# One written order of 340 steps for attention and the first two experts

## The chip, the cores and the metric

The kernel runs on one core of a Trainium2 chip. A core has five engines, each with its own queue of instructions: TensorE (PE, matmuls; its weight loads are shown as PEld), VectorE (DVE), ScalarE (ACT), GpSimd (Pool) and SyncE (SP). Sixteen DMA engines move data between the chip's memory and the core; Pool and SP start the transfers here. The metric is device time in microseconds (us), from the first to the last instruction of the run, median of several runs.

## The reference

Two operators in a row. First an attention without a score matrix, for 8 batches, 8 heads, 576 tokens and 64 dimensions a head:

```python
q_s = softmax(q, axis=-1)            # over the 64 dimensions
k_s = softmax(k, axis=2)             # over the 576 tokens
kv  = einsum('bhsd,bhse->bhde', k_s, v)
x   = einsum('bhsd,bhde->bhse', q_s, kv)   # then laid out as 4608 tokens x 512
```

Then a mixture of 8 experts over the 4608 tokens. Each token has one expert, fixed by its id; an expert is two matrices, 512 x 1024 and 1024 x 512:

```python
expert_idx = token_ids * 2654435761 % 8
for e in range(8):
    xe = x[expert_idx == e]
    out[expert_idx == e] = maximum(xe @ w1[e], 0) @ w2[e]
```

## The kernel before

**Slots.** Each expert has 640 slots of tokens: 72 for each of the 8 batches (columns 0 to 575), and 64 more (columns 576 to 639) for overflow, tokens of any batch that did not fit. DVE, PE and Pool first work out which token stands in which slot. Then the query rows of an expert are fetched in slot order, so that attention is computed already sorted by expert: five gathers of 128 rows (`raw`, L357, indices `gidx`), an exponential on ACT for each (`expq`, L368, into `qs`), sums and scales on DVE (`sums`, L380 to L386), transposes on PE (`turned`, L396) with a copy out of PSUM (L401, into `qT`), and products with the batch's key-value matrix `kvr` (`product`, L410) with a copy into the expert's input `XTp` or `X` (L413 on DVE, L415 on ACT). The overflow rows take the same way by indices `oidx`, with `xov` (L426) and a spread over the experts (`shared`, L436 to L444, into `XTov`).

**Keys and values.** For each batch SP loads `kraw` (L673), Pool loads `v` (L677, converted to 16 bits on the way); ACT takes the exponential of k (`expk`, L320) and fills v's extra columns with ones (`mark`, L324); PE makes 72 small matmuls (`keys`, L334); DVE scales the result into `kvr` (`scaled`, L341 to L347).

**An expert.** Its weights come in two halves for each matrix (`fetch`, L456). `first` (L471) makes steps of two blocks of 128 hidden units on some range of token columns, each followed by a relu on ACT into `hT` (L474); `second` (L482) makes a block of 128 tokens, DVE copies it to `ob` (L485), and Pool scatters its rows to the output (L488).

**Buffers.** Three `kraw`, four `v`, two k exponentials, ten `raw`, two `qs` sets, two weight sets, four `ob`. PSUM is held in three pairs: T for `keys`, `second` and overflow; Q for transposes and products; S (two banks each) for `first` and the spread.

**Order.** The block runs under a manual schedule for Pool, PE, DVE and ACT: every engine executes its instructions in the order in which the program names them. Expert 0 stands among the attention steps, its first matmul in three column ranges (0 to 288, 288 to 432, 432 to 640) as batches come. Experts 1 to 7 run in a loop, where small pieces for later experts are put after numbered steps by `_Slots`: softening of expert e+2, products of the next pair, exponentials of expert e+3. The gather of expert 3's queries is named after expert 0's last scatter, and its exponentials right behind:

```python
            for blk in range(3, BPE):
                moe.second(0, wts, hT, blk, opool, sl.side)
            qs[3] = gather(3)
            at.expq(qs[3], 0, 5)
```

Of the kernel before, what the change touches and what calls it, by code (L numbers as in the profile page):

```python
# [43 lines left out]
class _Index:  # L44
# [30 lines left out]
    def core(self, cpool, wait):  # L75
# [46 lines left out]
        A = ipool.tile([128, NCH, CELL], F16)  # L122
# [54 lines left out]
    def counts(self, cpool, fpool):  # L177
# [20 lines left out]
        flag = fpool.tile([128, 1], I32)  # L198
# [12 lines left out]
        return flag  # L211
# [17 lines left out]
    def onehot(self):  # L229
        V, Z = self.nc.vector, self.Z  # L230
        AO = self.ipool.tile([128, NCH, OVF], F16)
        V.tensor_tensor(out=AO[:], in0=self.rowi[:, 1:1 + OVF].unsqueeze(1).to_broadcast([128, NCH, OVF]),
                        in1=Z[:, 2, :].unsqueeze(2).to_broadcast([128, NCH, OVF]), op=ALU.is_equal)
        self.AO = AO

# [34 lines left out]
    def rows(self, cpool):  # L270
        nc, V = self.nc, self.nc.vector
        p2 = self.ps.tile([128, 512], F32, tag="T")
        for e in range(E_MOE):
            for n in range(NBP):
                nc.tensor.matmul(p2[64:128, 2 * e:2 * e + 2], lhsT=self.Qs[n][:, OVF * e:OVF * e + OVF],
                                 rhs=self.part[:, n, :], start=(n == 0), stop=(n == NBP - 1))
        u = slice(64, 128)
# [11 lines left out]
class _Attention:  # L289

    def __init__(self, nc, tc, q, k, v, cpool, qpool, ps):
# [11 lines left out]
        self.turn = 0  # L303
# [3 lines left out]
    def clear(self, lo, hi):  # L307
        for b in range(lo, hi):
            self.nc.vector.memset(self.kvrs[b][:], 0.0)

    def fill(self, ix):
        V = self.nc.vector
        V.tensor_scalar(out=self.ident[:], in0=ix.rowi[:, 0:128], scalar1=ix.pidf[:, 0:1], scalar2=None,
                        op0=ALU.is_equal)
        for i in range(2):
            V.memset(self.q16s[i][64:128, BPE - 1], 1.0)
# [33 lines left out]
    def gather(self, idx, widths):  # L350
        nc = self.nc
        q16 = self.q16s[self.turn % 2]
        self.turn += 1
# [36 lines left out]
    def turned(self, rq16, i, dst, act=False):  # L390
        nc = self.nc
        q16, w = rq16[1], rq16[2][i]
        pq = self.ps.tile([128, 512], F32, tag="Q")
        pv = pq[:].bitcast(F16).rearrange("p (r t) -> p r t", r=8)[:, 0:NPAIR, :]
        for r in range(NPAIR):
            nc.tensor.transpose(pv[:, r, 0:w], q16[0:w, i, 2 * r:2 * r + 2, :].rearrange("p h d -> p (h d)"),  # L396
                                self.ident[0:w, 0:w])
        if act:
            nc.scalar.copy(dst, pv[:, :, 0:w])
        else:  # L400
            nc.vector.tensor_copy(dst, pv[:, :, 0:w])  # L401

    def product(self, qT, XTp, r, lo, hi, es, q0=0):
# [8 lines left out]
        if r % 2:  # L412
            nc.vector.tensor_copy(XTp[:, es, r, lo * CELL:hi * CELL], pv)  # L413
        else:
            nc.scalar.copy(XTp[:, es, r, lo * CELL:hi * CELL], pv)  # L415

    def overflow(self, n, qTo, tpool):
# [7 lines left out]
        xov = tpool.tile([128, D_MOE], F16, name=f"xov{n}")  # L425
        nc.vector.tensor_copy(xov[:], pt[:])  # L426
        return xov

    def shared(self, xovs, Qs):
        nc = self.nc  # L430
        for h in range(2):
            pr = self.ps.tile([128, 2, 512], F32, tag="S")
            for i in range(2):
                r = 2 * h + i
                for n in range(NBP):
                    nc.tensor.matmul(pr[:, i, :], lhsT=xovs[n][:, r * 128:(r + 1) * 128], rhs=Qs[n][:],  # L436
                                     start=(n == 0), stop=(n == NBP - 1))
            for i in range(2):
                dst = self.XTov[:, :, 2 * h + i, :]
                src = pr[:, i, :].rearrange("p (e i) -> p e i", e=E_MOE)  # L440
                if i:
                    nc.scalar.copy(dst, src)
                else:
                    nc.vector.tensor_copy(dst, src)  # L444


class _Moe:
# [15 lines left out]
    def first(self, e, w, XTp, hT, lo, hi, side):  # L463
        nc = self.nc
        w1r = w[0][:].rearrange("p (c f) -> p c f", c=DC)
        for f2 in range(FC // 2):
            ph = self.ps.tile([128, 2, 512], F32, tag="S")
            for i in range(2):
                fc = 2 * f2 + i
                for dc in range(DC):  # L470
                    nc.tensor.matmul(ph[:, i, :hi - lo], lhsT=w1r[:, dc, fc * 128:(fc + 1) * 128],  # L471
                                     rhs=XTp[:, e % 2, dc, lo:hi], start=(dc == 0), stop=(dc == DC - 1))
            hv = hT[:, 2 * f2:2 * f2 + 2, lo:hi]
            nc.scalar.activation(hv, ph[:, :, :hi - lo], ACT.Relu)  # L474
            side()

    def second(self, e, w, hT, blk, opool, side):
# [3 lines left out]
        for fc in range(FC):  # L481
            nc.tensor.matmul(po[:], lhsT=hT[:, fc, blk * 128:(blk + 1) * 128], rhs=w2r[:, fc, :],  # L482
                             start=(fc == 0), stop=(fc == FC - 1))
        ob = opool.tile([128, D_MOE], F32, tag="ob")
        nc.vector.tensor_scalar(out=ob[:], in0=po[:], scalar1=1.0 / SX, scalar2=None, op0=ALU.mult)  # L485

        def scatter():
            sc = nc.gpsimd.indirect_dma_start(  # L488
                out=self.out[:, :],
                out_offset=bass.IndirectOffsetOnAxis(ap=self.ix.sidx[:, e, blk:blk + 1], axis=0),  # L490
                in_=ob[:], in_offset=None, bounds_check=N_TOK - 1, oob_is_err=False)
            self.tc.declare_no_dep(sc.ins, group="scatter", reason="each row is in one slot")
            self.tc.add_to_no_dep_group("scatter", sc.ins)
        scatter()
        side()
# [121 lines left out]

class _Slots:
# [21 lines left out]
def kernel(  # L640
# [10 lines left out]
    nc = tc.nc  # L651
    fpool = ctx.enter_context(tc.tile_pool(name="flag", bufs=1))
    with ExitStack() as fctx:
# [3 lines left out]
        xpool = P("xt", 2)  # L657
        qpool = P("q")
        wa = P("w16a", reuse_waits="tile")
        hpool = P("h")  # L660
        opool = P("o", 4)
        actx = ExitStack()
        tpool = P("tab", c=actx, side="right")
# [4 lines left out]

        kraws, v16s = {}, {}

        def load_k(b):
            kraws[b] = apool.tile([128, NPAIR * C9 * DH_], F32, tag="kraw", name=f"kraw{b}", bufs=3)
            nc.sync.dma_start(kraws[b][:], k[b])  # L673

        def load_v(b):
            v16s[b] = apool.tile([128, NPAIR * C9, VW], F16, tag="v16", name=f"v16_{b}", bufs=4)
            nc.gpsimd.dma_start(v16s[b][:].rearrange("p c d -> p (c d)"), v[b])  # L677

        QW = [128] * (BPE - 1) + [MAINC - 128 * (BPE - 1)]
        eng = mybir.EngineType  # L680
        with tc.manual_schedule(engines={eng.Pool, eng.PE, eng.DVE, eng.Activation}):
            at = _Attention(nc, tc, q, k, v, cpool, qpool, ps)
            at.clear(0, 4)
# [7 lines left out]
            gather = lambda e: at.gather(ix.gidx[:, e, :], QW)  # L691
            k16s, pkvs = {}, {}
            qT = qpool.tile([128, NPAIR, 4, MAINC], F16)

# [5 lines left out]
            def mark(b):  # L700
                at.mark(v16s[b])

            def keys(b):
                pkvs[b] = at.keys(k16s[b], v16s[b])

            def scaled(b):
                at.scaled(b, pkvs[b], apool)

            def turned(rq, e, i):
                at.turned(rq, i, qT[:, :, e % 4, 128 * i:128 * i + QW[i]])  # L710

            def turned_o(n):
                at.turned(qo, n, qTo[:, :, n * 128:(n + 1) * 128])

            ix.core(cpool, lambda: at.clear(4, 6))
            q0 = gather(0)
            load_v(2)
            load_v(3)
            expk(0)
            mark(0)  # L720
            keys(0)
            expk(1)
            at.clear(6, 8)
            flag = ix.counts(cpool, fpool)
            ix.overflow()
            scaled(0)
            ix.onehot()
            mark(1)
            keys(1)
            expk(2)  # L730
            at.expq(q0, 0, 3)
            scaled(1)
            po = ix.find()
            at.expq(q0, 3, 5)
            mul = at.sums(q0, 0, 3)
            ix.found(po, oidx, tpool)
            qo = at.gather(oidx, [128] * NBP)
            wts = moe.new_weights(wa)
            moe.fetch(wts, 0, 1)
            load_v(4)  # L740
            at.fill(ix)
            mul()
            Qs = ix.onehots(tpool)
            for i in range(3):
                turned(q0, 0, i)
            mark(2)
            keys(2)
            expk(3)
            ix.rows(cpool)
            at.soften(q0, 3, 5)  # L750
            scaled(2)
            load_v(5)
            moe.fetch(wts, 0, 2)
            for i in range(3, 5):
                turned(q0, 0, i)
            mark(3)
            keys(3)
            expk(4)
            at.expq(qo, 0, 4)
            scaled(3)  # L760
# [175 lines left out]
```

## Time and profile before

| | |
|---|---|
| runs | 272.69, 273.97, 274.76 us; median 273.97 |
| span of the profiled run | 270.1 us |
| busy: PE, PEld, DVE, ACT, Pool | 201.0, 131.8, 151.2, 102.9, 115.5 us |
| bytes moved by DMA | 51.42 MB, mean 190 GB/s |
| last key product (`keys`) | starts at 81.6 us |
| first matmul of expert 2 | at 145.8 us |

Engines overlap, so the busy times don't add up to the span. In the page's slices a digit is the busy share of one fortieth of the span in tenths; PEclk is the clock that PE was granted, in tenths. An idle time "[9.47 <-DMA raw]" is the time that the engine stood idle before this instruction, with what released it.

### The profile page before, as it was taken

The page shows a single profiled execution, that of the slowest core. Times are in us where ns is not written, and L with a number is a line of the kernel's source. Part 1 is how long each engine was busy: PE and PEld are TensorE (multiplying, and loading weights), DVE is VectorE, ACT ScalarE, POOL GpSimd, SP SyncE. Part 2 cuts the span into 40 slices and gives each one's busy share as a digit, 9 for nine tenths or more (in the row PEclk, how much of TensorE's full clock was granted, in tenths as well). Part 3 has the DMA queues.
Part 4 walks back from the last instruction along what each step waited for, and adds up shares of the span by engine and source line. Part 5 has one row for each costly group of instructions (what it writes and reads, how often), then busy time and mean ns, then how long its engine had stood idle before and what let it go on. Part 6 is the DMA issues. An engine that isn't in the chain of part 4 may idle for free. (4 is left out here: it accounts for less than half of the span.)

```text
span 270.1 us, 4969 instructions
## 1 busy us (share of the span) xinstructions
PE 201.0 (74%) x1987; PEld 131.8 (49%) x1987; DVE 151.2 (56%) x303; ACT 102.9 (38%) x159; POOL 115.5 (43%) x140
## 2 busy tenths in 40 slices
PE   2436084497925677707989999959999989999990
PEld 2435073275605525404656746635755745746640
DVE  8994747766279439416357846645954855022031
ACT  2334264155540343034435526525625532622500
POOL 5170393232741000487135857743874333434051
PEclk9999999999997579975999999999999999999999
DMA  6999989999996000179922997993798892793032
GB/s 251 312 343 372 285 244 305 258 212 287 217 291 178 0 4 0 65 184 197 274 84 91 179 275 220 201 293 123 147 226 298 159 223 100 141 227 134 27 115 73
DMA packets 13548, 51.42 MB, mean 190 GB/s; under 512 B 2504, under 2 KB 2504, under 8 KB 12496
## 3 DMA queue, kind: packets, MB, share of 16 engines
q0 software_dynamic: 12224, 41.58, 61.7%
q1 hardware_dynamic: 1296, 9.47, 9.1%
q8 instruction: 17, 0.28, 0.4%
q14 instruction: 11, 0.09, 0.1%
HBM read 63.25 MB, written 10.49 MB: 273 GB/s over the span
## 5 line engine op out<-in xcount | busy, mean ns | idle before, releaser
L488 POOL DMA_INDIRECT out_dram<-ob,sidx x40 | 40.2, 1005 | 99.0 <-DVE ob L485 95.6
L482 PE MATMUL po<-w2r,hT 128*128 128x512 f16 x320 | 73.4, 379 | 0.4 <-DVE kvr L347 0.4
L471 PEld LDWEIGHTS <-w1r 128*128 128x128 f16 x544 | 52.9, 101 | 34.7 <-issue 11.6
L474 ACT ACTIVATE hT<-ph 128x640 f16<-128x640 f32 (+3 forms) x68 | 45.5, 671 | 49.7 <-PE ph L471 49.6
L485 DVE TENSOR_SCALAR ob<-po 128x512 f32<-128x512 f32 x40 | 27.7, 692 | 57.3 <-PE po L482 54.3
L357 POOL DMA_INDIRECT raw<-in_q_dram,gidx x40 | 45.0, 1124 | 29.2 <-DVE row L162 7.9
L471 PE MATMUL ph<-X,w1r 128*128 128x320 f16 x384 | 54.5, 299 | 0.0
L482 PEld LDWEIGHTS <-hT 128*128 128x128 f16 x320 | 30.2, 98 | 32.5 <-issue 0.4
L368 ACT ACTIVATE qs<-raw 128x512 f16<-128x512 f32 (+1 forms) x44 | 26.5, 627 | 37.7 <-DMA raw<-in_q_dram,gidx 35.2
L380 DVE TENSOR_REDUCE rq<-qs 128x16 f32<-128x1024 f16 (+1 forms) x18 | 26.1, 1449 | 17.6 <-ACT qs L368 17.6
L471 PE MATMUL ph<-XTp,w1r 128*128 128x320 f16 (+3 forms) x160 | 24.2, 311 | 13.6 <-ACT hT L474 9.7
L396 PE MATMUL pq<-ident,qs 128*128 128x128 f16 (+1 forms) x176 | 17.2, 234 | 17.2 <-DVE qs L386 15.8
L386 DVE TENSOR_TENSOR qs<-qs,rq 128x1024 f16<-128x1024 f16 (+1 forms) x18 | 26.2, 1458 | 0.4
L334 PE MATMUL pt<-v,k 64*64 64x65 f16 x576 | 15.0, 223 | 13.5 <-ACT v L324 7.3
L396 PEld LDWEIGHTS <-qs 128*128 128x128 f16 (+1 forms) x176 | 13.1, 107 | 22.2 <-ACT v L324 10.2
L410 PE MATMUL px<-qT,kvr 128*128 128x144 f16 (+1 forms) x160 | 15.0, 232 | 9.4 <-ACT X L415 3.1
L334 PEld LDWEIGHTS <-k 64*64 64x64 f16 x576 | 14.4, 137 | 14.6 <-issue 13.7
L401 DVE COPY qT<-pq 128x512 f16<-128x512 f16 (+1 forms) x40 | 14.7, 389 | 9.7 <-PE pq L396 9.4
L320 ACT ACTIVATE k<-kraw 128x2304 f16<-128x2304 f32 x8 | 17.0, 2122 | 6.4 <-DMA kraw<-in_k_dram 4.5
L410 PEld LDWEIGHTS <-kvr 128*128 128x128 f16 x160 | 11.5, 108 | 14.4 <-issue 9.4
L415 ACT CAST X<-px 128x432 f16<-128x432 f32 (+1 forms) x18 | 8.6, 477 | 21.7 <-PE px L410 21.7
L413 DVE CAST X<-px 128x432 f16<-128x432 f32 (+1 forms) x18 | 9.9, 551 | 4.4 <-PE px L410 4.4
(103 smaller groups left out, 120.6 us busy)
## 6 DMA issues: line engine op xcount, KB each, us to landing
kraw<-in_k_dram SPq DMA_DIRECT2D x8, 1152.0 KB, 10.8
w1r<-in_moe_w_dram POOLq DMA_DIRECT2D x16, 512.0 KB, 7.3
w2r<-in_moe_w_dram POOLq DMA_DIRECT2D x16, 512.0 KB, 10.8
v<-in_v_dram POOLq DMA_DIRECT2D x8, 594.0 KB, 16.9
raw<-in_q_dram,gidx POOLq DMA_INDIRECT x40, 10.1
out_dram<-ob,sidx POOLq DMA_INDIRECT x40, 2.8
raw<-in_q_dram,oidx POOLq DMA_INDIRECT x4, 7.4
ids<-in_moe_token_ids_dram SPq DMA_DIRECT2D x1, 36.0 KB, 1.7
```

The source lines that it names most:

```text
L334: nc.tensor.matmul(pkv[s, r, 0:DH_ + 1], lhsT=k16[s, r * C9 + c, :], rhs=v16[s, r * C9 + c, 0:DH_ + 1], start=(c == 0), stop=(c == C9 - 1))
L357: nc.gpsimd.indirect_dma_start(out=raw[0:w, :], out_offset=None, in_=self.q[:, :], in_offset=bass.IndirectOffsetOnAxis(ap=idx[0:w, i:i + 1 ...
L368: self.nc.scalar.activation(q16[0:w, i].rearrange("p h d -> p (h d)"), raws[i][0:w, :], ACT.Exp)
L380: nc.vector.reduce_sum(rv, qv, axis=AX.X)
L386: nc.vector.tensor_tensor(out=qf, in0=qf, in1=rv.rearrange("p i h -> p (i h)").unsqueeze(2) .to_broadcast([w, (hi - lo) * H_, DH_]), op=AL ...
L396: nc.tensor.transpose(pv[:, r, 0:w], q16[0:w, i, 2 * r:2 * r + 2, :].rearrange("p h d -> p (h d)"), self.ident[0:w, 0:w])
L410: nc.tensor.matmul(pv[:, :, i * CELL:(i + 1) * CELL], lhsT=self.kvrs[b][:, r, :], rhs=qT[:, r, q0 + es.start:q0 + es.stop, b * CELL:(b + 1 ...
L471: nc.tensor.matmul(ph[:, i, :hi - lo], lhsT=w1r[:, dc, fc * 128:(fc + 1) * 128], rhs=XTp[:, e % 2, dc, lo:hi], start=(dc == 0), stop=(dc = ...
L474: nc.scalar.activation(hv, ph[:, :, :hi - lo], ACT.Relu)
L482: nc.tensor.matmul(po[:], lhsT=hT[:, fc, blk * 128:(blk + 1) * 128], rhs=w2r[:, fc, :], start=(fc == 0), stop=(fc == FC - 1))
L485: nc.vector.tensor_scalar(out=ob[:], in0=po[:], scalar1=1.0 / SX, scalar2=None, op0=ALU.mult)
L488: sc = nc.gpsimd.indirect_dma_start(out=self.out[:, :], out_offset=bass.IndirectOffsetOnAxis(ap=self.ix.sidx[:, e, blk:blk + 1], axis=0), ...
```

## The change

All of attention and of experts 0 and 1 is cut into named steps, and one list gives their order; each engine executes its part of the list. A name tells the step: EK, MK, KV, SC are `expk`, `mark`, `keys` and `scaled` of a batch; V a load of v; G a gather (GO of the overflow rows); EQ an exponential of one query tile; SM and ML the sum and the scale; TP and TC a transposed tile and its copy; PP and PC a product and its copy; XP and XC the overflow product and its cast; SH and SD the spread; OV the overflow columns of a pair; W a weight matrix; A and R a step of `first` and its relu; B, C and S a block of `second`, its copy and its scatter. CNT, OVA, OHA, FND, FDD, QS, ROP and ROD make the index of the overflow.

What it is for: work of one expert can stand between pieces of another, so that an engine that waits for one has the other. Both experts now have their first matmul in two column ranges, 0 to 288 and 288 to 640. v's third load stands ahead of the first gather, the gathers of experts 2 and 3 follow each other, the overflow gather is named before the sums of expert 0, and DVE reaches its index without them. Copies of transposed tiles of experts 0, 1 and the overflow, the overflow casts, and the clearing of `kvr` and `qs` move from DVE to ACT. The second weight set and its pool are there from the start. Experts 2 to 7 keep their loop.

```diff
-    def clear(self, lo, hi):
-        for b in range(lo, hi):
-            self.nc.vector.memset(self.kvrs[b][:], 0.0)
+    def clear(self):
+        nc = self.nc
+        zero = self.cpool.tile([128, 1], F16, name="zero")
+        nc.vector.memset(zero[:], 0.0)
+        for b in range(B_):
+            nc.scalar.copy(self.kvrs[b][:].rearrange("p r d -> p (r d)"), zero[:].to_broadcast([128, NPAIR * 128]))
+        for i in range(2):
+            nc.scalar.copy(self.q16s[i][64:128, BPE - 1].rearrange("p h d -> p (h d)"),
+                           self.two[64:128, 0:1].to_broadcast([64, D_MOE]))
...
+ORDER = """
+EK0 MK0 V2 CNT KV0 G0 EK1 OVA SC0 MK1 KV1 OHA EK2 V3 V4 SC1 FND MK2 FDD KV2 EK3 QS GO EQ0_1 ROP SC2 EQ0_0 EQ0_2
+EQ0_3 SM0a EQ0_4 EK4 W01 ROD V5 ML0a G1 SM0b TP0_2 TP0_1 TC0_2 TC0_1 TP0_0 MK3 ML0b TC0_0 KV3 TP0_4 SC3 EK5 V6
+TP0_3 V7 W02 TC0_4 MK4 W11 PP0_00 TC0_3 KV4 PC0_00 EQO_0 W12 EQO_1 PP0_01 SC4 EK6 PP0_03 SMOa EQO_3 EQO_2 PC0_01
+MLOa PP0_02 G2 PC0_02 SMOb TPO_0 TCO_0 TPO_1 PC0_03 XP0 TCO_1 MLOb A0_0_1 XC0 A0_0_3 R0_0_1 TPO_3 R0_0_3 TPO_2
+A0_0_0 MK5 EQ1_0 KV5 EQ1_1 R0_0_0 EQ1_4 EQ1_3 A0_0_2 SC5 EK7 XP1 SM1b MK6 ML1b XC1 KV6 R0_0_2 EQ1_2 MK7 G3 SM1a
+TCO_3 KV7 TCO_2 ML1a TP1_3 TP1_4 TC1_3 TC1_4 SC6 TP1_2 TP1_1 TC1_2 SC7 TC1_1 XP2 TP1_0 XC2 PP0_40 XP3 TC1_0
+PC0_40 B0_0 XC3 PP1_01 C0_0 PP1_41 SH1 PC1_01 S0_0 PC1_41 PP0_42 SD1 PP1_42 SH0 PC1_42 PC0_42 PP0_43 SD0 PP0_41
+B0_1 EQ2_0 PC0_41 OV0 EQ2_1 PC0_43 EQ2_2 PP1_02 C0_1 PP1_00 EQ2_3 A0_288_0 SM2a S0_1 PC1_02 EQ3_1 A0_288_2 EQ3_2
+ML2a PC1_00 PP1_03 R0_288_2 PP1_43 R0_288_0 A0_288_1 PC1_43 EQ3_3 PC1_03 TP2_2 EQ3_0 OV1 TP2_0 R0_288_1 TC2_2
+A1_0_2 TC2_0 EQ3_4 SM3a A0_288_3 R1_0_2 EQ2_4 PP1_40 W21 A1_0_0 R0_288_3 ML3a TP2_1 PC1_40 G4 B0_2 R1_0_0 TC2_1
+SM2b A1_288_3 TP3_1 R1_288_3 C0_2 TP3_0 B0_3 ML2b TC3_1 A1_288_0 C0_3 S0_2 TC3_0 TP2_4 SM3b R1_288_0 S0_3 PP2_03
+B0_4 TC2_4 ML3b PP2_02 W22 A1_288_1 PC2_02 PC2_03 TP3_2 C0_4 R1_288_1 TP2_3 A1_0_1 TC3_2 EQ4_3 S0_4 TC2_3 EQ4_4
+PP2_01 TP3_3 EQ4_2 PC2_01 A1_0_3 TC3_3 R1_0_1 PP2_00 TP3_4 R1_0_3 A1_288_2 TC3_4 PC2_00 EQ4_0 PP2_61 PP2_60
+R1_288_2 PC2_61 B1_0 EQ4_1 PC2_60 PP2_62 C1_0 PP2_30 PC2_62 B1_2 PC2_30 S1_0 PP2_31 C1_2 PP2_32 B1_3 PC2_31
+PC2_32 S1_2 PP2_33 C1_3 PP2_63 B1_1 PC2_33 S1_3 PC2_63 B1_4 C1_1 S1_1 C1_4 S1_4
+""".split()
...
+                            A(qTo[:, :, i * 128:(i + 1) * 128], pq[e, i])
+                        else:
+                            (A if e < 2 else V)(qT[:, :, e % 4, 128 * i:128 * i + QW[i]], pq[e, i])
...
+                (V if r % 2 else A)(X[:, es, r, lo * CELL:hi * CELL], px[e, r, lo])
+
+            for e, es, parts in ((0, slice(0, 1), ((0, 4), (4, 8))), (1, slice(1, 2), ((0, 4), (4, 8))),
+                                 (2, slice(0, 2), ((0, 3), (3, 6), (6, 8)))):
...
+            for e in (0, 1):
+                for lo, hi in ((0, 288), (288, CAP)):
...
+            for name in ORDER:
+                st.run(name)
...
-            qs[3] = gather(3)
-            at.expq(qs[3], 0, 5)
...
-            for e in range(1, E_MOE):
-                wts = wn
...
+            for e in range(2, E_MOE):
+                h, w = hs[e % 2], wts[e]
```

Here A stands for ACT's copy and V for DVE's.

## The prediction

> **What bounds the kernel now.** I read the page's busy row and slices first, then the busy table by stages, then the waits of PE in the stage with the holes, and last the order of time on ACT and Pool around the largest hole. The chain of waits is no help: it holds only the last 0.7 us.
>
> ```profile
> PE 201.0 (74%) x1987; PEld 131.8 (49%) x1987; DVE 151.2 (56%) x303; ACT 102.9 (38%) x159; POOL 115.5 (43%) x140
> PEclk9999999999997579975999999999999999999999
> DMA  6999989999996000179922997993798892793032
> ```
>
> No engine is full over the span, and DMA has a hole of zeros where PE's clock is also down. So the stages differ. Cut at the points where the work changes:
>
> ```profile
> 0.00:57.00 57.00, 26.02 (x511) 22.32 (x512) 41.63 (x112) 19.51 (x22) 23.86 (x40) 1.00 0.97 292
> 57.00:69.00 12.00, 10.07 (x215) 7.18 (x214) 7.81 (x19) 6.83 (x9) 3.82 (x6) 1.00 1.05 256
> 69.00:84.00 15.00, 8.45 (x191) 6.60 (x190) 8.23 (x14) 6.54 (x12) 8.38 (x9) 0.90 1.04 255
> 84.00:146.00 62.00, 43.11 (x310) 26.54 (x308) 32.07 (x59) 21.08 (x40) 19.11 (x20) 0.83 0.37 99
> 146.00:270.00 124.00, 113.33 (x768) 69.19 (x766) 61.45 (x102) 48.97 (x77) 60.35 (x66) 1.00 0.70 175
> ```
>
> Columns: window, length, busy PE, PEld, DVE, ACT, Pool, granted clock, DMA share, GB/s. Until 84 us the 16 DMA engines are full (0.97 to 1.05): that stage is DMA-bound. From 84 to 146 DMA is at 0.37 and PE has 18.9 us of idle time, with a clock of 0.83: neither is full, so this is a stage of bad order. From 146 (experts 2 to 7) PE is 91% busy at full clock. Which waits make the 18.9 us:
>
> ```profile
> PE ph L471 <- ACT hT L474: 9.7, 1, 9.7
> PE pq L396 <- DVE qs L386: 1.8, 1, 1.8
> PE ph L471 <- DVE XTp L826: 1.7, 1, 1.7
> ```
>
> One wait is half of it. PE waits for a relu; the relu's own queue shows why it is late, and Pool shows why its blocker is late:
>
> ```profile
> 116.76 0.63 ACT L368 ACTIVATE qs<-raw 128x512 f16<-128x512 f32 x1 [9.47 <-DMA raw<-in_q_dram,gidx]
> 122.56 1.27 ACT L474 ACTIVATE hT<-ph 128x640 f16<-128x640 f32 x2
> ```
>
> ```profile
> 109.99 0.98 POOL L488 DMA_INDIRECT out_dram<-ob,sidx  x1 [26.63 <-DVE ob L485]
> 111.95 0.98 POOL L488 DMA_INDIRECT out_dram<-ob,sidx  x1 [0.98 <-DVE ob L485]
> 113.24 1.05 POOL L357 DMA_INDIRECT raw<-in_q_dram,gidx  x1 [0.30 <-issue]
> ```
>
> The five exponentials of expert 3's queries stand in ACT's order ahead of expert 1's relus; their gather stands in Pool's order behind the scatters of expert 0's last two blocks, which wait for their results. So Pool sat 26.6 us while DMA was idle, then ACT 9.5 us for the gather, then PE 9.7 us for ACT.
>
> [...] after the hole from 113.6 to 123.3 the clock is 0.50 until 128, and 32 matmuls of 320 columns take 7.21 us, against 48 in 6.68 us later. [...]
>
> **The change, part by part.**
>
> 1. *Loads reordered.* Bytes are the same; what counts is what stands ahead of the last attention batch. Cost per load, in time of all 16 engines: the SP queue has 9.1% of 270.1 us for eight k loads, 24.6 us. In the stretch from 50 to 58 us almost only weights move, at about 215 GB/s, so a half of 0.52 MB is 2.45 us and a matrix 4.9. The two late stages (0.37 x 62 = 22.9 us; 0.70 x 124 = 86.8 us) hold 4 and 20 halves, 2 and 3 gathers of five, about 1.4 and 6 sets of five scatters, and some 1.5 us of earlier work; solved, a gather set costs about 2 us and a scatter set about 5. The 82 us before 84 then leave 27 us for the eight v loads. The new Pool order puts ahead of v's last load: v 27, k 24.6, gathers of expert 0, overflow and expert 1 6, w1 of expert 0 4.9: 62.5 us, with 3 us of start and 1.5 of gaps 67. The old order also had w2 of expert 0 before it and issued v's last load only at 61.5 us, after a gather whose issue waited for landings; the last key product ran at 81.6 to 83.8. New: load at about 66, product of 72 matmuls 1.34 (warm, against 2.19 cold) to about **68**. Gain at this point about 16 us, but work that was done before it moves behind it.
>
> 2. *PE work left after the last key product.* Durations of busy rows at full clock: B (second matmul, 8 of 512 columns) 1.79 (24 took 5.36): 10 blocks 17.9. A (first matmul): 48 of 320 columns took 6.68, 0.139 each, 64 an expert: expert 1 8.9, and the upper 352 of 640 columns of expert 0 4.9. Spread of the overflow rows, 16 of 512 columns: 3.6 (5.48 in the cold stage of before). Transposes: 15 tiles x 0.39 = 5.9. Attention products: 12 of four matmuls x 0.32, 12 of three x 0.28: 7.1. Two overflow products 0.8. Sum **49 us**. Before, the stage after 83.8 held 43.1 us busy plus 18.9 idle, which makes 145.7, where expert 2 starts.
>
> 3. *The expert 3 gather moved up*, behind expert 2's and before the first scatter. The five v, w1, w2 and gather sets up to it sum to 67 + 14.7 (three matrices) + 4 = 86 us; Pool's issue of ten gathers at 1.3 us apart (13 us) can add a little: landing 86 to 90. ACT's new order has two of its exponentials just ahead of the first relu of expert 0's upper part. PE comes there after 5 transposed tiles, 4+5 products, two overflow products, the spread and B blocks 0 and 1, 13 us after 68, with round trips 83 to 86. The wait of 9.7 us is gone; about **3 us** of a like wait take its place, with A steps and everything after them queued behind it.
>
> 4. *Expert 2's w1 and expert 4's gather* stand on Pool behind the last A step of expert 0's columns (about 93) and scatters 0 and 1. Issue of five gathers 6.6 us, w1 4.9 of DMA before them: landed about 104. ACT takes the first exponential after some 18 us more of PE work, at 108. Hidden, with 4 us to spare; if not, the relus of expert 1 wait.
>
> 5. *Copies moved to ACT*: eight clears and two fills at the start, 14 tile copies, four overflow casts. No row shows a clear on ACT; bounded by 0.58 (cast of 512 columns) and 0.63 (exponential of 512). I take 0.6: ten end at about 8, not 6.6, so the first k exponential is 1.4 late; hidden, since v's first load lands at 13.4. Further 18 x 0.6 = 11 us on ACT, which until 84 is busy 33 us. DVE loses about 12 us. Zero on the path.
>
> 6. *Overflow gather early*: it waited for indices until 31.4, because DVE stood 4.4 us on a sum ahead of them. Now about 26. DMA is full there, so this by itself is worth nothing but the order.
>
> 7. *DVE after 86*: sums and scales of experts 2 and 3 (13.6 us) with copies, results and casts give some 21 us in the 22 us until 108: nearly full, and transposes wait for it. With two psum buffers for transposes and products alike, I put **6 us** on such waits from 68 to the end (before: the 18.9 idle less 9.7 is 9.2).
>
> Experts 2 to 7 keep their loop: 270.1 - 145.7 = **124.4**. Sum: 68 + 49 + 3 + 6 = 126 for the start of expert 2; 250.4 span. The median of the timed runs is 3.9 above the profile's span: **254**.
>
> **Rivals.** (a) *Waits fully hidden*: 68 + 49 + 2 = 119, 243 span, 247. For: the loop of experts 2 to 7 shows that interleaved products hide their copies. Against: DVE's load in point 7 and the gather in point 3. (b) *A convoy of another kind*: one more queue blocked, by an exponential ahead of a relu or by a transposed tile, costs like the old one 10 us, and half clock after it some 3 more: 139, 267. For: one order for four engines holds many such pairs, and points 3 and 4 have margins of few us. (c) *Slower*: the last key product doesn't come earlier (Pool still stalls on landings, 84), 49 us of work stay behind it, and both late gathers block (two waits of 10, 4 of half clock): 157, 281 span, 285. For: Pool's gathers in this trace waited up to 3.4 us for weights to land. Against: the bytes ahead of v are fewer, and a blocked Pool means only that the DMA engines have work.
>
> **How the numbers follow.** As worked out (250 to 260): 0.58; (a) 0.17; (b) 0.13; (c) and near-equal outcomes 0.12. Bounds of the unknowns: last key product 65 to 72, waits 2 to 18 us. That gives 246 to 268, leaving out the worse half of (b) and (c). Faster by over 1%: 0.86; within 1%: 0.03; slower: 0.11.
>
> **What would show it.** Right: the last key product at 65 to 70; DMA full past 84 until about 95; Pool's 26.6 us wait gone; no PE wait over 5 us after 70; expert 2's first matmul at about 126; the loop after it 124 us long. Wrong: ACT's exponentials waiting over 5 us for a gather with relus behind; PE clock at 0.5 after 84; DVE over 95% busy with PE waiting for transposed tiles; v's last load after 72.

## The result and the profile after

The changed kernel takes **246.84 us** (four runs, 246.38 to 247.28) against 274.37 for the kernel before on the same chip (272.69 to 275.43): a ratio of 0.900 [0.895, 0.905]. The forecast was 254.0 with a range of 246 to 268. The profiled run spans 244.5 us. Now and then an execution takes some per cent longer than the others of its kernel: medians below are of all runs, ratios leave those out. (The written list has 287 names, not the 340 of the title.) The page of the profiled run has, for the three lines shown of before:

```profile
PE 195.6 (80%) x1955; PEld 128.0 (52%) x1955; DVE 139.2 (57%) x274; ACT 114.4 (47%) x181; POOL 113.8 (47%) x140
...
PEclk9999999999998999999999999799999999999998
DMA  6999999999999728795599499529988924982032
```

The three zeros in DMA are gone, and of the 5s and 7s in PE's clock one 7 is left, in the loop. Now the busy time by stages (columns as in the prediction: window, length, busy PE, PEld, DVE, ACT, Pool, clock, DMA share, GB/s):

```profile
0.00:57.00 57.00, 26.81 (x582) 23.83 (x583) 38.23 (x102) 32.16 (x42) 22.59 (x42) 1.00 0.99 310
57.00:69.00 12.00, 9.49 (x267) 7.54 (x265) 6.65 (x12) 9.69 (x18) 6.18 (x8) 1.00 1.06 219
69.00:84.00 15.00, 12.59 (x104) 7.10 (x105) 8.78 (x20) 7.01 (x16) 6.87 (x7) 0.89 0.99 252
84.00:120.00 36.00, 34.94 (x265) 22.02 (x264) 27.79 (x48) 19.01 (x36) 20.76 (x22) 1.00 0.63 168
120.00:244.50 124.50, 111.73 (x744) 67.50 (x741) 57.81 (x95) 46.55 (x73) 57.42 (x63) 0.98 0.69 171
67.80:116.46 48.66, 44.55 (x349) 26.90 (x349) 34.43 (x65) 25.35 (x48) 25.82 (x26) 0.96 0.77 198
86.00:108.00 22.00, 21.38 (x174) 14.13 (x174) 18.49 (x33) 14.19 (x26) 12.99 (x13) 1.00 0.68 167
```

The sixth row is the stage that the prediction worked out: from the last key product to the first matmul of expert 2. PE is busy for 44.55 of 48.66 us, 92%. The same stage of the kernel before, between its own two points, was 70% busy:

```profile
83.80:145.77 61.97, 43.08 (x310) 26.55 (x309) 32.01 (x60) 20.92 (x39) 19.11 (x20) 0.83 0.37 100
```

Expert 2 starts 29.3 us earlier (116.46 against 145.77). Counted from the start of the span to that point, PE's busy time fell from 87.4 to 80.3 us (the mean granted clock to that point is 0.99 and was 0.92, and 32 matmuls fewer by the two pages, 1955 against 1987) and its idle time from 58.4 to 36.2. The waits of PE from 60 to 130 us that are left:

```profile
PE pq L399 <- DVE qs L389: 2.1, 1, 2.1
PE pt L338 <- ACT v L328: 1.9, 2, 1.5
PE px L410 <- ACT XT L810: 0.7, 1, 0.7
...
PE ph L462 <- ACT hT L467: 0.4, 1, 0.4
```

No wait is over 2.1 us; the 9.7 us for a relu is 0.4. The order of time on ACT and on Pool shows the pair of queues that made it:

```profile
84.64 1.28 ACT L371 ACTIVATE qs<-raw 128x512 f16<-128x512 f32 x2 [0.32 <-DMA raw<-in_q_dram,gidx]
85.82 0.38 ACT L810 CAST XT<-px 128x288 f16<-128x288 f32 x1
86.10 1.41 ACT L467 ACTIVATE hT<-ph 128x704 f16<-128x704 f32 x2
```

```profile
83.01 0.95 POOL L360 DMA_INDIRECT raw<-in_q_dram,gidx  x1 [0.30 <-ACT qs L371]
84.27 1.03 POOL L484 DMA_INDIRECT out_dram<-ob,sidx  x1 [0.30 <-issue]
85.61 1.00 POOL L484 DMA_INDIRECT out_dram<-ob,sidx  x1 [0.30 <-DVE rq L384]
```

Expert 3's last gather is issued at 83.01, ahead of the first scatter, and the exponentials ahead of the relus wait 0.32 us where they waited 9.47.

The loop from expert 2 on got longer: 244.5 - 116.46 = 128.0 us against 124.3. The step from expert 3's first matmul to expert 4's is 27.4 us, against 23.7 before; expert 2's step is the same (18.55, 18.54). In it ACT and then PE wait:

```profile
133.19 0.63 ACT L371 ACTIVATE qs<-raw 128x512 f16<-128x512 f32 x1 [6.68 <-DMA raw<-in_q_dram,gidx]
...
153.32 0.63 ACT L371 ACTIVATE qs<-raw 128x512 f16<-128x512 f32 x1 [5.39 <-DMA raw<-in_q_dram,gidx]
```

```profile
154.41 0.88 PE L410 MATMUL px<-qT,kvr 128*128 128x144 f16 x6 [3.46 <-ACT XT L810]
155.09 3.14 PE L474 MATMUL po<-w2r,hT 128*128 128x512 f16 x8
...
158.44 1.89 PE L474 MATMUL po<-w2r,hT 128*128 128x512 f16 x8
```

An exponential waits for its gather, a copy stands behind it on ACT, and PE waits 3.46 us for the copy. The eight matmuls after that take 3.14 us, at a granted clock of 0.50 from 154.4 to 157.5; the same eight take 1.89 us at 158.44, where it is 1.00. The length of the wait does not tell which it will be: the kernel before has this wait too, at 2.29 us, and the eight matmuls after it took 1.89 us; in b_g3 (below) it is 1.82 us, and they took 3.18. What decides is open.

### The profile page after: what moved, and what is told of

The parts are those of the page before. It is cut to its first block, busy times and chain, and to the rows that moved or that the text cites. A ratio compares the mean times of both kernels' runs of the same rounds, so it can differ in the third digit from the quotient of the medians.

```text
span 244.5 us, 4885 instructions
## 1 busy us (share of the span) xinstructions
PE 195.6 (80%) x1955; PEld 128.0 (52%) x1955; DVE 139.2 (57%) x274; ACT 114.4 (47%) x181; POOL 113.8 (47%) x140
## 3 DMA queue, kind: packets, MB, share of 16 engines
q1 hardware_dynamic: 1296, 9.47, 9.8%
## 4 chain that ended last, share of the span: by engine, by line
PE 49%; DMA 33%; issue 5%; DVE 5%; POOL 3%; ACT 2%; POOLq 0%; ACTq 0%; DVEq 0%
PE ph L462 22%; PE po L474 22%; DMA raw<-in_q_dram,gidx 17%; DMA v<-in_v_dram 9%; DMA w2r<-in_moe_w_dram 7%; PE px L410 3%; PE pq L399 2%; POOL raw L360 2%; DVE A L127 1%; ACT qs L371 1%; ACT hT L467 1%; DVE ob L480 1%; ACT XT L810 1%; DVE EV L107 0%; POOL w1r L448 0%
## 5 line engine op out<-in xcount | busy, mean ns | idle before, releaser
L462 PE MATMUL ph<-XT,w1r 128*128 128x320 f16 (+2 forms) x512 | 75.6, 303 | 1.1 <-ACT hT L467 1.1
L474 PE MATMUL po<-w2r,hT 128*128 128x512 f16 x320 | 75.3, 387 | 0.0
L467 ACT ACTIVATE hT<-ph 128x640 f16<-128x640 f32 (+2 forms) x64 | 44.8, 703 | 43.4 <-PE ph L462 43.2
L462 PEld LDWEIGHTS <-w1r 128*128 128x128 f16 x512 | 49.8, 99 | 21.3 <-issue 1.6
L399 PE MATMUL pq<-ident,qs 128*128 128x128 f16 (+1 forms) x176 | 16.4, 228 | 12.8 <-DVE qs L389 11.9
L399 PEld LDWEIGHTS <-qs 128*128 128x128 f16 (+1 forms) x176 | 12.3, 103 | 17.0 <-issue 10.3
L810 ACT CAST XT<-px 128x288 f16<-128x288 f32 (+1 forms) x26 | 11.6, 453 | 20.5 <-PE px L410 20.4
L810 DVE CAST XT<-px 128x288 f16<-128x288 f32 (+1 forms) x26 | 13.2, 518 | 6.8 <-PE px L410 6.8
L448 POOL DMA_DIRECT2D w1r<-in_moe_w_dram x16 | 9.3, 596 | 7.2 <-PE px L410 4.7
L448 POOL DMA_DIRECT2D w2r<-in_moe_w_dram x16 | 8.9, 576 | 2.3 <-DMA v<-in_v_dram 1.6
```

Source lines behind the costliest of these rows:

```text
L399: nc.tensor.transpose(pv[:, r, :], q16[0:w, i, 2 * r:2 * r + 2, :].rearrange("p h d -> p (h d)"), self.ident[0:w, 0:w])
L467: self.nc.scalar.activation(hT[:, 2 * f2:2 * f2 + 2, lo:hi], ph[:, :, :hi - lo], ACT.Relu)
L810: (V if r % 2 else A)(X[:, es, r, lo * CELL:hi * CELL], px[e, r, lo])
```

## The experiments

My theory at the start was that the gain is a sum of two causes: loads in a better order (the last key product earlier) and the early gather of expert 3 (the hole closed), with the rest small. The rival: neither helps much in the old order of steps, and the gain comes from steps of two experts standing between each other. Names that begin with b_ are the kernel before with one edit, with a_ the changed kernel with one edit. Each is compared with the kernel before on the same chip (275.12, 276.02 and 274.78 us for the three groups).

### Only the early gather, in the old order: b_g3

```diff
             at.expq(qs[1], 0, 5)
+            qs[3] = gather(3)
...
-            qs[3] = gather(3)
             at.expq(qs[3], 0, 5)
```

> The kernel before, with one line moved: the gather of expert 3's queries is named right after expert 1's exponentials, before the third scatter; its exponentials stay where they are. Mine (the hole and the load order each gave their part): the 26.6 us wait on Pool and the 9.7 us wait of PE go, and the half clock after them; 12 to 14 us less, 260 to 262. Rival 1 (this hole is nearly all of the gain): 250 or less. Rival 2 (DMA is full and only shifts): under 4 us less.

Measured: 270.33 us, ratio 0.982 [0.975, 0.990]. The hole is gone: from the start of expert 1 to that of expert 2 it takes 25.5 us (117.46 to 143.00), not 35.0. But expert 1 starts 6.7 us later than before (110.78). So two thirds of the gain were lost ahead of it: the last key product ran from 83.38 to 90.5, in pieces with gaps that the trace puts down to "issue" (time in which an engine waits for nothing that the profile shows), where before it ran from 81.64 to 83.83. All three expectations missed.

### Only the load order, in the old order: b_load

```diff
-            moe.fetch(wts, 0, 2)
...
-            load_v(6)
...
+            load_v(6)
...
+            moe.fetch(wts, 0, 2)
```

v's load 6 goes behind the gather of expert 1, and w2 of expert 0 behind v's loads 6 and 7.

> The kernel before with the new order of loads alone: w2 of expert 0 behind v of batches 6 and 7, v 6 behind the gather of expert 1. Mine, as forecast: the last key product, which starts at 81.6, comes some 5 us earlier and the run is 3 to 6 us shorter. Rival (the last key product waited for DVE's and ACT's order of steps and not for its load): it stays within 1 us of 81.6, and the run within 1.5 us of the kernel before, or longer, because w2 of expert 0 now lands later.

Measured: 286.75 us, 1.046 [1.039, 1.053]: slower. PE's order of time:

```profile
69.74 1.89 PE L482 MATMUL po<-w2r,hT 128*128 128x512 f16 x4 [1.81 <-DMA w2r<-in_moe_w_dram]
...
91.63 2.50 PE L334 MATMUL pt<-v,k 64*64 64x65 f16 x72 [5.91 <-DVE kvr L347]
```

The last key product ran later, at 91.6 us, not earlier. PE's order has blocks of expert 0's second matmul ahead of it; they need w2, which now came later (that line stands at 64.43 before). So the earlier v brought nothing here: its consumer stood behind something that needs what was put back. The rival had named this way of getting longer, though not its size.

### Both of them: b_both

The edits of b_g3 and b_load together.

> The kernel before with both: the gather of expert 3 early and the new order of loads. Mine: 16 to 20 us less, 254 to 258, which leaves about 8 to the finer order of steps. Rival (the order of loads is worth nothing unless the steps are interleaved): the same as with the gather alone, 260 to 262, and 13 or more left to the interleaving.

Measured: 278.68 us, 1.013 [1.005, 1.022]. The gather takes 8 us off b_load, but the two together are slower than the kernel before. Both expectations missed: the sum of two causes was not there to be had.

### Load order with the key steps moved up: b_keys_load

b_load, and the steps of the last two batches named early, so that nothing that needs w2 stands ahead of them:

```diff
             scaled(5)
+            mark(6)
+            keys(6)
+            expk(7)
+            scaled(6)
+            mark(7)
+            keys(7)
+            scaled(7)
...
-            mark(6)
-            keys(6)
-            expk(7)
...
```

> The kernel before with the new order of loads and, on top, the last two batches' key products (with their marks, exponentials and scales) named right after batch 5's, ahead of expert 0's second matmul. The gather of expert 3 stays late. If the last key product was late because of the steps named ahead of it (blocks that need w2, sums on DVE) and not because of its load: it now ends at 67 to 71 instead of 84, and the run is 6 to 14 us shorter than before, 261 to 269, with the 9.7 us hole still there. If loads and steps don't matter for the end, since the same work is only shifted: within 3 us of the kernel before.

Measured: 280.57 us, 1.017 [1.011, 1.023]. The last key product now ends at about 70.6 us, 13 us earlier, and yet expert 1 starts at 111.76 against 110.78. The busy table of this kernel between those points shows why:

```profile
70.70:84.00 13.30, 8.57 (x72) 4.88 (x70) 7.13 (x13) 4.79 (x11) 3.58 (x5) 1.00 1.02 258
84.00:111.76 27.76, 18.30 (x145) 11.78 (x145) 18.63 (x34) 7.80 (x17) 1.78 (x2) 0.75 0.04 16
```

Over 41 us PE is busy for 27 (65%), with DMA at 0.04 in the second row. The old order has a chain of softening, transposes, products and copies of expert 0 there, and nothing of another expert beside it: PE waits 6.3 us for softened queries and 2.9 for transposed tiles. So the key product came when it was expected (67 to 71), and the 261 to 269 us did not: alone, with nothing to put into these gaps, the earlier product bought nothing.

### The gather a little later: b_g3_after

The early gather cost b_g3 its key product, so it stands behind that here:

```diff
             keys(7)
+            qs[3] = gather(3)
...
-            qs[3] = gather(3)
```

> The kernel before with the gather of expert 3 named behind the last key product, so that Pool issues it after the third scatter, at about 83, and not ahead of it. In the run with the gather earlier the last key product took from 83.4 to 90.5 instead of 2.2 us, in pieces of a few matmuls with nothing that they waited for in the trace. If that came from the gather's transfers beside it: here the product takes 2.2 us again, the hole of expert 1 is gone as well, and the run is 9 to 13 us shorter than before, 261 to 265. If the hole itself is worth only 5 us: 269 to 271 again.

Measured: 270.53 us, 0.981 [0.974, 0.987], the same as b_g3; the expected 261 to 265 missed. The 269 to 271 of the other expectation came, but not for its reason: the hole is gone (25.6 us from expert 1 to expert 2, not 35.0), and expert 1 starts at 117.50 again. PE and then DVE of this kernel in order of time:

```profile
82.70 2.34 PE L334 MATMUL pt<-v,k 64*64 64x65 f16 x65 [4.59 <-DMA w2r<-in_moe_w_dram]
85.46 0.33 PE L334 MATMUL pt<-v,k 64*64 64x65 f16 x4 [0.43 <-issue]
...
86.92 1.22 PE L396 MATMUL pq<-ident,qs 128*128 128x128 f16 x7 [0.21 <-issue]
92.58 0.59 PE L396 MATMUL pq<-ident,qs 128*128 128x128 f16 x4 [4.45 <-DVE qT L401]
```

```profile
92.10 0.75 DVE L401 COPY qT<-pq 128x512 f16<-128x512 f16 x2 [5.93 <-remote]
```

Before, the third transposed tile follows at 85.50 and here at 92.58: all 7 us are lost in this stretch, 1.1 by a later start, 2.4 in pieces, 3.6 in PE's wait for a DVE copy. DVE made that copy at 92.10, when its tile had been complete since 88.1 at the latest ("remote" is a release whose sender the trace does not name). The five gathers were issued from 84.73 to 90.95, and their queue kept the DMA engines 57 to 67% busy from 86 to 92, where before it was 11% from 86 to 88 and nothing from there to 92. Why PE and DVE stand still meanwhile is open. One candidate, the loading of instructions, speaks against itself: the page lists it as a DMA queue of its own (17 packets, 0.28 MB), but its only packet from 76 to 95 us lies between 82 and 84, ahead of DVE's gap.

### The old load order in the new steps: a_loadold

```diff
-... EK2 V3 V4 SC1 ... EK4 W01 ROD V5 ML0a ... V7 W02 TC0_4 ...
+... EK2 V3 SC1 ... EK4 W01 V4 ROD V5 W02 ML0a ... V7 TC0_4 ...
```

> The changed kernel with two loads moved back to where they were: v of batch 4 behind w1 of expert 0, and w2 of expert 0 behind v of batch 5, ahead of expert 1's gather and v of batches 6 and 7. All else the same. If the bytes ahead of the last v load set the last key product (4.9 us more of them): it ends at about 72 instead of 67.8 and the run is 3 to 5 us longer, 250 to 252. If the order of steps alone matters: within 1.5 us of 246.8.

Measured: 254.21 us, 0.920 [0.912, 0.928]. The last key product ends at 74.9 us and expert 2 starts at 123.36, 48.4 us after it (48.7 in the changed kernel). So with interleaved steps a later last key product moves the start of expert 2 along with it: by 6.9 us, and the runs by 7.4, against the first measurement; by 3.6 and 3.9 against the control further on (after_again), whose interval of the ratio overlaps this one. The way it goes is that of the first expectation; the size isn't settled.

### The copies back on DVE: a_dve

```diff
-    A(qTo[:, :, i * 128:(i + 1) * 128], pq[e, i])
+    V(qTo[:, :, i * 128:(i + 1) * 128], pq[e, i])
...
-    (A if e < 2 else V)(qT[:, :, e % 4, 128 * i:128 * i + QW[i]], pq[e, i])
+    V(qT[:, :, e % 4, 128 * i:128 * i + QW[i]], pq[e, i])
...
-    A(xovs[n][:], po["x", n][:])
+    V(xovs[n][:], po["x", n][:])
```

> The changed kernel with the copies of transposed tiles of experts 0 and 1 and of the overflow, and the four overflow casts, back on DVE at their places in the order; the clears stay on ACT. Mine: up to 84 us both engines have room, so within 1.5 us of the changed kernel, 245 to 249. Rival (DVE's relief was part of the gain): DVE gets some 9 us more in a stretch where key scales and sums stand in its order, the last key product or the transposes after it come later, 3 us or more longer, 250 and up.

Measured: 253.84 us, but the four runs (251.38, 251.84, 255.85, 257.15) lie too far apart for a ratio. Expert 2 starts at 121.56, 5.1 us later than in the first measurement and 1.8 later than in the control. DVE is busy for 21.01 of the 22 us from 86 to 108 (18.49 with the change), and PE waits for DVE copies: 1.7 and 0.9 us for `qT`, 0.7 for `xov`. Yet PE is busy for 21.15 of those 22 us (21.38 with the change); 3.9 of the 5.1 us were lost by the end of the last key product, 71.69 against 67.81. The direction is the rival's. By the two shorter runs the size is 4.5 to 5 us against the first measurement and 1 to 1.5 against the control, which is no more than noise: it isn't settled.

### The changed kernel again: after_again

No edit, on the chip of the three kernels below.

> The changed kernel as it is, as a measure for the three that run beside it on this chip and for the runs before. 246 to 250, a ratio to the kernel before of 0.895 to 0.905; the last key product at 66 to 69 and expert 2's first matmul at 115 to 119.

Measured: 250.34 us (248.89 to 251.15), 0.912 [0.905, 0.919]. All four expectations missed by a little. The last key product ends at about 70.5 us instead of 67.8 and expert 2 starts at 119.73 instead of 116.46, so most of the difference between the two profiles, 2.7 of 3.3 us, is there by the end of that product. Whether the chip makes it is open: a_mix (below, same chip, same steps up to there) ended its last key product at 67.6 and still began expert 2 at 118.64. The control sets the grain: between groups, 3.5 us mean nothing.

### Expert 3's gather later in the new steps: a_g3late

```diff
-... KV6 R0_0_2 EQ1_2 MK7 G3 SM1a
+... KV6 R0_0_2 EQ1_2 MK7 SM1a
...
-... SM2a S0_1 PC1_02 ...
+... SM2a S0_1 G3 PC1_02 ...
```

> The changed kernel with the gather of expert 3 named behind expert 0's second scatter and no longer ahead of the first; its exponentials stay ahead of the relus of expert 0's upper columns. Pool issues it from about 87 to 93, not 75 to 83. If the place of the gather matters in the new order as it did in the old: ACT waits 6 to 9 us for it, PE for the relus behind, and the run is 5 to 10 us longer than the changed kernel. If PE's order holds enough other work there: under 2 us longer.

Measured: 258.96 us, but the four runs (254.69, 258.82, 259.10, 261.11) lie too far apart for a ratio; the profile is of the one of 259.10. Even the shortest run is 4.4 us above the control's median and 3.5 above its longest. The wait itself is plain in the waits of PE and ACT from 60 to 130 us:

```profile
PE px L410 <- ACT XT L810: 7.8, 1, 7.8
```

```profile
ACT qs L371 <- DMA raw<-in_q_dram,gidx: 7.4, 2, 6.6
```

The old convoy, one queue held up behind another, is back, with a copy in the relu's place. Expert 2 starts at 129.62 (control 119.73). Undoing the move costs 4.4 us by the shortest run, more by the others.

### Gathers ahead of weights in the loop: a_loop

This and the two below ask for the 3.7 us that the loop lost. Here each gather of the loop is issued before the next weights:

```diff
+                if e + 3 < E_MOE:
+                    qs[e + 3] = gather(e + 3)
                 if e + 1 < E_MOE:
...
-                    qs[e + 3] = gather(e + 3)
```

> The changed kernel, with one thing moved in the loop of experts 2 to 7: the gather for expert e+3 is issued before the weights of expert e+1. The stretch from expert 2's first matmul to the end was 128.0 us after the change and 124.3 before, and the difference is all in expert 3 (27.4 against 23.7 us), where ACT waits for gathers ahead of relus and copies. If the late landing of gathers behind weights is the cause: expert 3 takes about 19 to 22 us, and the run is 5 to 8 us shorter, 239 to 242. If it is the DMA engines being full, whatever the order: within 2 us of 246.8, since weights land later by as much.

Measured: 260.57 us, 0.944 [0.931, 0.958]: slower than the changed kernel. ACT's waits for gathers from 115 to 250 us fall from 19.1 to 1.1 us, but DVE now waits 18.7 us for result buffers (1.2 in the changed kernel), and PE 11.0 us for queries that DVE softens behind these waits. Both expectations missed. One of DVE's three waits:

```profile
144.25 0.69 DVE L480 TENSOR_SCALAR ob<-po 128x512 f32<-128x512 f32 x1 [7.21 <-DMA out_dram<-ob,sidx]
```

Four scatters were issued behind the weights, from 132.5 to 138.3, and read the four `ob` buffers; the fifth result has none until one of them is through. The first of the four, issued at 132.52 behind weights issued from 129.94, lets DVE go on only at 144.25: here a scatter behind weights held its source for 11.7 us, where a scatter of the changed kernel takes 3.2 us from issue to landing (median; 8.5 at most).

### The same with six result buffers: a_loop_ob

```diff
-        opool = P("o", 4)
+        opool = P("o", 6)
```

> The gather ahead of the weights in the loop of experts 2 to 7, as in the run that came out at 260.6, but with six result buffers and not four. In that run DVE stood 18.7 us in three waits for a result buffer, whose scatter stood in Pool's queue behind the weights' transfers; with the changed kernel it was 1.2 us. If these waits are what made it slower: they go or halve, the gathers are as early as there, and the run comes to 240 to 246. If something else (the weights' landing) made it slower: 257 or more again.

Measured: **243.60 us** (242.63 to 243.98), 0.888 [0.882, 0.894]. That is better than both kernels: 6.7 us below the changed one on the same chip, whose interval it doesn't touch. Its waits of DVE and of ACT from 115 to 250 us:

```profile
DVE ob L480 <- DMA out_dram<-ob,sidx: 1.1, 1, 1.1
```

```profile
ACT qs L371 <- DMA raw<-in_q_dram,gidx: 0.7, 2, 0.4
```

Both waits are gone at once. Expert 2 starts at 119.50 as in the control, and the loop takes 122.0 us (control 129.2); expert 3's step is 21.95. The first edit alone looked like a loss of 10 us; six buffers without it were not tried. DVE's waits for buffers in the changed kernel, 1.2 us (4.4 in the control), leave less to gain there than the 6.7 us.

### The gather between the two matrices: a_mix

Four result buffers, and the gather after w1 and ahead of w2.

> The changed kernel with the gather for expert e+3 between the two weight matrices of expert e+1 in the loop: half of the weights' bytes ahead of the gather, half behind it and ahead of the scatters. If the two costs (gathers behind weights, scatters behind weights) trade off evenly: 243 to 248. If the scatters' side is the dearer one: 250 to 256.

Measured: 248.25 us (246.81 to 251.74), 0.905 [0.898, 0.913]. Part of each wait is left from 115 to 250 us: 7.3 us of DVE for scatters, 3.9 of ACT for gathers. Expert 3's step is 22.9. The run lies at the upper end of the first expectation; against the control's 0.912 it is within the intervals.

## Why the prediction was right, and where it wasn't

The time fell into the range, 7 us under the forecast. The sum of the prediction and what was measured for it: the start of expert 2 at 126 against 116.46, the loop 124.4 against 128.04, median over span 3.9 against 2.3. That is -9.5 + 3.6 - 1.6 = -7.5 on 254.3, which gives 246.8. That it stayed in the range is in part luck: it lies 0.8 us above the lower end, outside the 250 to 260 that had the greatest chance, and without the loop's loss of 3.6 us it would have been below. It is rival (a)'s 247, but made of other parts (44.55 + 4.1 us, not 49 + 2).

**1, loads.** The last key product was forecast to end at 68 and ended at 67.8. v's last load, issued at 53.78, landed at about 65 (66 was forecast), and ACT's own order then let the product begin at 66.47, so a small part of the agreement is luck. What failed is the account of the old kernel, which put its late product down to v's last load. The trace of before shows it waiting for DVE:

```profile
81.64 2.19 PE L334 MATMUL pt<-v,k 64*64 64x65 f16 x72 [5.91 <-DVE kvr L347]
```

With the loads alone moved it came later (b_load); with its steps moved too it came 13 us earlier, for no gain at the end (b_keys_load). Only in the new order does the start of expert 2 follow it (a_loadold).

**2, work left.** 49 us against 44.55 busy. The list of work was right, the sum was not: it added the lengths of rows, and the rows of different lines overlap. Summed by line, PE's rows in this window give 51.4 us (second 19.7, first 15.1, products 6.7, transposes 5.0, spread 3.8, overflow products 1.1), but they cover only 44.55. How far a short kind overlaps what follows, the trace of before shows:

```profile
153.60 0.39 PE L396 MATMUL pq<-ident,qs 128*128 128x128 f16 x4
153.82 1.25 PE L471 MATMUL ph<-X,w1r 128*128 128x320 f16 x8
```

A transposed tile is 0.39 us long, but the next row starts 0.22 us after it: an estimate of 3.3 us for 15 tiles, where the prediction took 5.9. The 43.1 busy us of the old stage are no measure either: they hold 7 blocks of the second matmul and not 10, and run in part at half clock (0.50 from 123.3 to 128). This term is half of the 9.5 us.

**3 and 7, waits.** Forecast 3 + 6 = 9 us, measured 48.66 - 44.55 = 4.1: the other half. Expert 3's gather was through in time (0.32 us of ACT, 0.4 of PE for a relu). DMA, forecast full until about 95, was at 0.04 from 88 to 90 and at 0 from 90 to 92. DVE was 84% busy from 86 to 108 (18.49 of 22), not nearly full; and that a nearly full DVE makes PE wait failed too, for in a_dve it had 21.01 us of work there and PE was still busy for 21.15. Here rival (a) was nearer: it had expert 2 at 119.

**4.** Right: ACT takes expert 4's first exponential at 102.9 without a wait.

**5.** Right for ACT. "Zero on the path" is not confirmed: a_dve is 1 to 5 us slower, which isn't clear of the noise.

**6.** The overflow gather came at 26.26 us, as forecast. It was not tried alone; that it is worth nothing by itself stays argued.

**The loop.** Taking it over unchanged was wrong by 3.6 us. The loop's code is the same, but ACT's waits for gathers rose from 16.7 to 19.1 us, and PE paid in three places of expert 3's step: a wait for a copy of 3.46 and not 2.29 us, half clock after it (0.50 from 154.4 to 157.5, some 1.5 us), and a wait for a relu of 0.77 us that was not there before. So two of the prediction's signs of being wrong, an exponential that waits over 5 us for its gather and half clock after 84 us, did appear, in the stage that it had taken over. Why the gathers come later there is open. a_loop_ob shows that these waits can go, and more: its loop is shorter than that of before.

**The cause.** My theory of two added causes fell: in the old order the loads alone cost 4.6%, the loads with the key steps moved up 1.7%, and the gather brings 1.8%. What b_keys_load lacks and the changed kernel has is work of another expert in the gaps of the first: PE is busy for 92% of the time from the last key product to expert 2, where the kernel before has 70%. Loads, key steps and gather together were not tried in the old order. An estimate from b_keys_load: without its wait of 9.49 us for the relu, and with the 32 matmuls after it in 4.52 us as in b_g3 and not in 6.94, its 280.6 us become 269, still 22 above the changed kernel. Within the new order the early gather is worth 4.4 us or more. The loads (4 to 7) and DVE's relief (1 to 5) point the same way, but were only compared across chips, and are not clear of the grain of 3.5 us. That the rest comes from the interleaving is argued, not shown: it was not tried without the three, nor were the two column ranges in place of three and the earlier overflow gather tried by themselves.

## What to carry to other kernels

In these runs a load that came earlier, or a hole that was closed, was worth only what the order of the consumers let through (ratios of 1.046 for b_load, 1.017 for b_keys_load, 0.982 for b_g3): look at what stands ahead of the consumer on its own engine, and at what will fill the time it frees. Where two engines waited for transfers that Pool issues, moving one kind ahead moved the wait to the other (a_loop: ACT's from 19.1 to 1.1 us, DVE's from 1.2 to 18.7), and two more buffers took away both (0.7 and 1.1 us, a_loop_ob): pair the move with as many buffers as the transfers put back will hold. Price a kind of matmul by the time from its start to the start of the next, where nothing waits (0.22 us for a transposed tile here), and not by the length of its row (0.39).

## What was not expected of the hardware

Scatters behind weights in Pool's queue held their buffers so long (11.7 us for one) that DVE waited 18.7 us in three waits with four buffers (a_loop), and 1.1 us with six (a_loop_ob). While gathers were being issued at 84 to 91 us (b_g3_after), PE's small matmuls ran with gaps of 0.2 to 0.4 us put down to "issue", and DVE stood 5.9 us with nothing that the trace shows to wait for; in the changed kernel, with gathers and full DMA (0.99) at 69 to 84 us, the trace lists no wait of PE for "issue" between 60 and 100 us, though other runs of that order have one or two, 0.7 us in the control. What tells them apart is open. The same kernel took 246.8 us on one chip and 250.3 on another, where the kernel before hardly differed (274.4 and 274.8).
